# Two buffers for the last weight tiles, and another order of filter loads and reads, in a spectral filter and MLP mixer kernel

## The chip, the cores and the metric

The kernel runs on one core of one Trainium2 chip. The metric is the device time of one execution in microseconds (us), as a median of several executions. The engines of the core are TensorE (PE in the profile, with PEld for its weight loads), VectorE (DVE), ScalarE (ACT), GpSimd (POOL) and SyncE (SP). SP, ScalarE and GpSimd issue DMA transfers. [...]

## The reference

All arrays are float32 in the kernel; `x` is (8, 3008, 256). First a filter along the sequence, done in frequency space, then an MLP mixer: a token part over the 3008 positions and a channel part over the 256 channels.

```python
X = np.fft.rfft(x, axis=1)                       # n_freq = 1505
y = np.fft.irfft(X * (filt_r + 1j * filt_i)[None], n=3008, axis=1)

xt = y.transpose(0, 2, 1)
h = np.maximum(xt @ w_tok1, 0.0) @ w_tok2        # 3008 -> 256 -> 3008
u = y + h.transpose(0, 2, 1)
h2 = np.maximum(u @ w_ch1, 0.0) @ w_ch2          # 256 -> 1536 -> 256
out = u + h2
```

The weights arrive as 64-bit numbers and are turned into float32 on the chip.

## The kernel before, in words

**The filter.** The length 3008 is 47 x 64. For each batch, length-64 transforms are matmuls against a table `wa` or `was` (`a_unit`, `a_pair`); their results z are copied out of PSUM by ScalarE (L517) and written to a DRAM scratch `z_tmp` (L519). Then, for 16 chunks `c` of two frequencies, `b_pair` (L501 with `wb`) does the length-47 transforms from a tile `t2` of z read back (L601, L602), multiplies by the filter tile `filts[c % 3]` on VectorE (L644), `join` adds the parts (L649, L650), and `bi_pair` does the inverse (L501 again), whose result goes to another scratch, `g_tmp` (L659). The batches go through this in five groups: batch 0 alone, then (1, 2), (3, 4), (5, 6) and (7). Each group is a Python generator, `dft`, that yields after each small step. Where a group changes over from the length-64 steps to the chunks, GpSimd clears part of each filter tile (L664), and the first two chunks' reads, tables (L548) and filter pieces (L215, L217: eight small transfers from the two filter arrays) are issued on SP. In group (1, 2) the z results are written from ScalarE's queue and the x tiles lie partly in the filter tiles; in the later groups SP writes z.

**The mixer.** `mix` runs over batches, six column blocks `m` and six hidden blocks `jp`; one such item is an up projection in seven half-block products (`up_first` L844, `up_last` L860), sums on VectorE (`up_middle`, L822), a ReLU on ScalarE (L865) and a down projection (L878). In `up_middle` VectorE needs a copy `s` that ScalarE makes of the first product (L847). The steps of the next group's `dft` are called between the parts of these items, at places written out by hand. So the order of work on each engine is the order in which this Python code issues it.

**The weights.** Each weight tile is a generator of four steps, taken one each by four iterators over the same list `tiles`: load into a staging tile `st`, a copy with a scale on ScalarE (L265), two instructions on VectorE (L267, L268), and two more with the sum into the weight (L271, L273, L295). One `convert()` call advances the third iterator, then the fourth, then `copies()` advances the second as far as its rule lets it, then `fill` starts loads. At this stage the third iterator is one tile ahead of the fourth. The last ten tiles (`LAST`) are taken in the first five items of `mix`, one call ahead of `up_middle` and one ahead of `up_last` in each item. Their loads come from GpSimd's queue (L372, L383), between the sums that GpSimd makes of the finished weights (L362 to L366). Before the change each of these tiles holds one buffer of pool `p1p` (`top`) and one of `p2p` (`rest`), which the filter's products use later.

Of the kernel before, what the change touches and what calls it, by code (L numbers as in the profile page):

```python
# [10 lines left out]
FP32 = mybir.dt.float32  # L11
# [12 lines left out]
P = 128  # L24
# [95 lines left out]
def kernel(  # L120
# [30 lines left out]
    def pool(name, bufs, **kw):  # L151
        return ctx.enter_context(tc.tile_pool(name=name, bufs=bufs, **kw))
# [6 lines left out]
    p1p = pool("p1p", 1)  # L159
    p2p = pool("p2p", 1)  # L160
# [96 lines left out]
    def halves(st, n, pair):  # L257

        words = [st.bitcast(t).rearrange("p (n w) -> p n w", w=2)[:, 0:n] for t in (U32, FP32)]
        lo, hi, hi_f = words[0][:, :, 0], words[0][:, :, 1], words[1][:, :, 1]  # L260
        top, rest = (v[:, 0:n] for v in pair)
        top_i, rest_i = top.bitcast(U32), rest.bitcast(U32)


        nc.scalar.activation(out=top, in_=hi_f, func=AF.Copy, scale=2.0 ** -112)  # L265
        yield
        nc.vector.tensor_scalar(out=top_i, in0=top_i, scalar1=3, scalar2=None, op0=ALU.logical_shift_left)  # L267
        nc.vector.scalar_tensor_tensor(out=top_i, in0=hi, scalar=0x80000000, in1=top_i,  # L268
                                       op0=ALU.bitwise_and, op1=ALU.bitwise_or)
        yield  # L270
        nc.vector.tensor_scalar(out=rest_i, in0=top_i, scalar1=0xFF800000, scalar2=None, op0=ALU.bitwise_and)  # L271

        nc.vector.scalar_tensor_tensor(out=rest, in0=lo, scalar=2.0 ** -52, in1=rest, op0=ALU.mult, op1=ALU.mult)  # L273
        yield top, rest
# [3 lines left out]
    def spare_pair():  # L278
        where, tag = spare[0]
        spare.append(spare.pop(0))  # L280
        both = where.tile([P, 2, 512], FP32, tag=tag, name="both")
        return both[:, 0], both[:, 1]

    def rounded(st, n, parts, late):
        if late:

            pair = (p1p.tile([P, 512], FP32, tag="p1", name="top"), p2p.tile([P, 512], FP32, tag="p2", name="rest"))
        else:
            pair = spare_pair()
        h = halves(st, n, pair)  # L290
        yield next(h)
        yield next(h)
        top, rest = next(h)
        for src, dst in parts:
            nc.vector.tensor_tensor(out=dst, in0=src(top), in1=src(rest), op=ALU.add)  # L295


    ended = [0]
# [14 lines left out]
    def w1_load(i):  # L313
        st = stage(512)
        rows = moe_w_tok1.rearrange("(n2 n1) t -> n2 n1 t", n1=N1)
        q = nc.sync if i < EARLY else nc.gpsimd
        last = 2 * i + 2 == A
        if last:
            nc.gpsimd.memset(st.bitcast(U32)[HALF:P, 512:1024], 0)
        for h in range(2):  # L320
            n = 1 if last and h else 2
            lo = h * A + 2 * i
            src = rows[:, lo:lo + n, :]
            if h == 0:
                src = bass.AP(tensor=rows.tensor, offset=rows.offset + (A - 1 - lo) * DT,
                              ap=[[N1 * DT, N2], [-DT, n], [1, DT]])
            q.dma_start(st[h * HALF:(h + 1) * HALF, 0:n * DT].rearrange("p (a t) -> p a t", t=DT), src)
        yield

        h = halves(st, 512, spare_pair())  # L330
        yield next(h)
        yield next(h)
        on_chip(wai_t, *next(h), 512, [(lambda v: v, w1[:, 2 * i:2 * i + 2, :].rearrange("p a t -> p (a t)"))])

    def w2_load(i):

        t, g = divmod(i, W2G)
        nn = min(NG, N2 - g * NG)
        n = nn * N1

        st = stage(512)
        nc.gpsimd.dma_start(st[:, 0:n], moe_w_tok2[ts(t, P), ds(g * NG * N1, n)])
        yield
        dst = w2[:, t].rearrange("p (a h n2) -> p h n2 a", h=2, n2=HALF)[:, :, ds(g * NG, nn), :]

        def some(h, first, step, w):
            return (lambda v: bass.AP(tensor=v.tensor, offset=v.offset + first, ap=[v.ap[0], [N1, nn], [step, w]]),
                    dst[:, h, :, 0:w])

        parts = [some(0, A - 1, -1, A), some(1, A, 1, A - 1)]  # L350
        if i < BY_PE:
            h = halves(st, n, spare_pair())
            yield next(h)
            yield next(h)
            on_chip(ident, *next(h), n, parts)
        else:
            yield from rounded(st, n, parts, False)
# [10 lines left out]
    def wc1_load(i, late=True):  # L368
        c, q = divmod(i, DC // 512)
        st = stage(512)  # L370
        for g in range(CB):
            nc.gpsimd.dma_start(st[ts(g, CW)], moe_w_ch1[ds((g * DH + c) * CW, CW), ts(q, 512)])  # L372
        yield

        yield from rounded(st, 512, [(lambda v: v.rearrange("p (i j n) -> p i j n", j=2, n=P),
                           chan[0][:, 2 * q:2 * q + 2, slice(0, 5, 4) if c == 0 else slice(1, 7, 5)])], late)
        if c == DH - 1:
            for jp in range(2 * q, 2 * q + 2):
                combine(chan[0][:, jp:jp + 1])

    def wc2_load(i):
        st = stage(512)
        nc.gpsimd.dma_start(st.rearrange("p (j d) -> p j d", d=D),  # L383
                            moe_w_ch2[ts(i, 2 * P), :].rearrange("(j p) d -> p j d", p=P))
        yield

        def tile_of(dh):
            return lambda v: v.rearrange("p (j g e i) -> p e j g i", j=2, e=DH, i=CW)[:, dh]

        yield from rounded(st, 512, [(tile_of(dh), chan[1][:, i, n].rearrange("p j (g i) -> p j g i", i=CW))  # L390
                          for dh, n in ((0, slice(0, 2)), (1, slice(4, 7, 2)))], True)
        combine(chan[1][:, i:i + 1])


    LAST = ((wc2_load, 0), (wc1_load, 1), (wc1_load, 4), (wc2_load, 1), (wc1_load, 2), (wc2_load, 2), (wc1_load, 5),
            (wc2_load, 3), (wc2_load, 4), (wc2_load, 5))

    tiles = ([w1_load(i) for i in range(A // 2)] + [w2_load(i) for i in range(TC * W2G)]
             + [wc1_load(c * (DC // 512), False) for c in range(DH)] + [f(i) for f, i in LAST])
    begin, copy, middle, end = (iter(tiles) for _ in range(4))  # L400

    def advance(it):
        s = next(it, None)
        if s:
            next(s, None)
# [14 lines left out]
    def convert_end():  # L420
        ended[0] += 1
        advance(end)
        copies()
        fill(5)

    copied = [0]

    def copies():

        while copied[0] < len(tiles) and copied[0] <= ended[0] + (copied[0] < len(tiles) - len(LAST)):  # L430
            advance(copy)
            copied[0] += 1

# [101 lines left out]
    def dft(bs):  # L535
        first = bs[0] == 0
# [5 lines left out]
        def table_load(c):  # L542
            if c * KC % WC == 0:
                g = c * KC // WC
                where, tag = (t1p, "t1") if first and g % 5 > 2 else (wbp, "wb")
                shape, src = ([P, WC, P + KR], wbi0_d[:, ts(g, WC), :]) if first else ([P, 4, HALF], wbi_d[:, g])
                wbs[g] = where.tile(shape, FP32, tag=tag, name="wb")
                nc.sync.dma_start(wbs[g], src)  # L548

        def w_load(c):  # L550
            table_load(c)
            (filt_load if first else filt_pair)(c)
# [38 lines left out]
        def t2_load(c):  # L591
            if first:
                return
            t2s[c] = t2p.tile([P, KC, nb, D], FP32, tag="t2", name="t2")
            for h in range(2):
                z = z_d[place_of[bs[0]][0]].rearrange("(e h k) a b d -> e h a k b d", e=2, h=2)
                for e in range(2):
                    to = t2s[c][ds(h * HALF + e * A, A)]
                    k = c == 0
                    if k:  # L600
                        nc.sync.dma_start(to[:, 0:1], z[h, e, :, 0:1])  # L601
                    nc.sync.dma_start(to[:, k:KC], z[e, h, :, c * KC + k:c * KC + KC])  # L602
# [59 lines left out]
        for c in range(FB):  # L662
            if not first:
                nc.gpsimd.memset(filts[c][:, :, 0, :], 0.0)  # L664
            if c < 2:
                t2_load(c)
                if not first:
                    w_load(c)
        yield "w"
        yield "b"  # L670
        if not first:
# [365 lines left out]
    with tc.manual_schedule():  # L1037
        nc.sync.dma_start(wa0, wa0_d)
        nc.vector.memset(turned[:, A:K2, :], 0.0)
        for t in filts:  # L1040
            nc.vector.memset(t, 0.0)
        half = 0
        second = dft(GROUPS[1])
        for i, _ in enumerate(dft(GROUPS[0])):
            if i == 0:
# [33 lines left out]
        both = wcp.tile([P, 2, JP, 7, P], FP32, tag="wc", name="wc")  # L1079
# [76 lines left out]
```

## Time and profile before

| | |
|---|---|
| median of 3 runs | 2497.85 us (2496.29 to 2501.91) |
| the profiled execution | 2499.35 us |
| its span, first to last instruction | 2497.6 us |
| TensorE busy | 2420.1 us (97%) |
| VectorE busy | 1846.7 us (74%) |
| ScalarE busy | 678.6 us (27%) |
| GpSimd busy | 598.4 us (24%) |
| mean granted TensorE clock | 0.993 |
| DMA | 236.07 MB, mean 95 GB/s |

In lines of a timeline the columns are start, duration, engine, line, operation, output and inputs, shape and count, and in brackets the idle time of the engine just before, with what ended it. In lines of waits: who waited for whom, then total us, number, longest. In lines of stretches of time: the stretch, its length, busy us of PE, PEld, DVE, ACT and POOL with counts, the granted clock, the share of the DMA engines that was busy, and GB/s.

### The profile page before, as it was taken

The numbers are of one execution on the slowest core, as the hardware profiler recorded it, in microseconds if no ns is written. First come the engines' busy times: TensorE is split into PE (matmuls) and PEld (weight loads), VectorE is DVE, ScalarE is ACT, GpSimd is POOL, SyncE is SP. The second block draws the span as 40 slices with busy tenths as digits, with TensorE's granted clock in tenths as the row PEclk, the third lists the DMA queues.
The fourth block names the chain that finished last, engine by engine and source line by source line (L and its number), as shares of the span: only waits on it lengthen the run. The fifth ranks groups of instructions, "written<-read, shape, count | busy, mean of one in ns | idle before, by whom it ended". The sixth has DMA issues, their size and how long they took to land.

```text
span 2497.6 us, 33945 instructions
## 1 busy us (share of the span) xinstructions
PE 2420.1 (97%) x11836; PEld 1962.4 (79%) x11836; DVE 1846.7 (74%) x3404; ACT 678.6 (27%) x1348; POOL 598.4 (24%) x1086
## 2 busy tenths in 40 slices
PE   7888999999999999999999999999999999999997
PEld 3556676877788777887778877897888888898887
DVE  7686878587885878667885788758786678757776
ACT  5633222133221222223221222213221222212221
POOL 6473332212111211211121112111212112212121
PEclk9999999999999999999999999999999999999999
DMA  9973444254321222335332323314322121301100
GB/s 217 252 206 118 123 131 144 76 170 131 109 82 53 82 82 61 94 99 172 89 94 62 86 71 83 103 45 126 86 77 72 49 70 43 98 24 29 39 16 18
DMA packets 173122, 236.07 MB, mean 95 GB/s; under 512 B 33213, under 2 KB 123067, under 8 KB 172952
## 3 DMA queue, kind: packets, MB, share of 16 engines
q1 hardware_dynamic: 128344, 175.53, 24.1%
q0 software_dynamic: 33376, 48.46, 7.8%
q10 hardware_dynamic: 11232, 9.92, 1.3%
q8 instruction: 94, 1.54, 0.3%
q14 instruction: 76, 0.62, 0.1%
HBM read 156.56 MB, written 77.22 MB: 94 GB/s over the span
## 4 chain that ended last, share of the span: by engine, by line
PE 44%; DVE 5%; issue 1%; DMA 0%; ACT 0%; DVEq 0%; POOL 0%; SPq 0%; ACTq 0%; POOLq 0%
PE ps_po L878 17%; PE ps_pg L844 10%; PE ps_pg L860 7%; PE ps_b L721 2%; PE ps_acc L721 2%; PE ps_b L765 2%; PE ps_acc L765 2%; DVE t L822 1%; DVE hh L822 1%; PE ps_acc L501 1%; DVE p L644 1%; PE ps_b L501 1%; PE ps_b L743 1%; PE ps_acc L743 1%; DVE s L822 1%
## 5 line engine op out<-in xcount | busy, mean ns | idle before, releaser
L925 POOL DMA_DIRECT2D out_dram<-r x757 | 412.5, 553 | 1672.4 <-ACT hh L865 1408.4
L822 DVE TENSOR_TENSOR hh<-ps_pg,s 128x512 f32<-128x512 f32 (+3 forms) x864 | 482.6, 586 | 390.2 <-ACT s L847 386.8
L865 ACT ACTIVATE hh<-hh 128x512 f32<-128x512 f32 (+1 forms) x576 | 348.3, 623 | 986.2 <-DVE hh L822 986.2
L878 PE MATMUL ps_po<-t,wc 128*128 128x256 f32 (+1 forms) x2304 | 546.6, 380 | 4.2 <-DVE t L822 3.1
L878 PEld LDWEIGHTS ps_po<-t,wc 128*128 128x128 f32 x2304 | 426.3, 190 | 132.4 <-DVE t L822 41.1
L844 PE MATMUL ps_pg<-v,wc 128*128 128x256 f32 (+1 forms) x1728 | 415.5, 377 | 2.1 <-DVE v L822 2.1
L878 PE MATMUL ps_po<-hh,wc 128*128 128x256 f32 (+1 forms) x1728 | 413.5, 375 | 0.2 <-ACT hh L865 0.2
L844 PEld LDWEIGHTS ps_pg<-v,wc 128*128 128x128 f32 x1728 | 327.8, 191 | 43.5 <-DVE v L822 5.9
L878 PEld LDWEIGHTS ps_po<-hh,wc 128*128 128x128 f32 x1728 | 329.1, 191 | 38.2 <-ACT hh L865 0.5
L860 PE MATMUL ps_pg<-u,wc 128*128 128x256 f32 (+1 forms) x1152 | 295.8, 379 | 6.0 <-DVE hh L822 6.0
L860 PEld LDWEIGHTS ps_pg<-u,wc 128*128 128x128 f32 x1152 | 215.5, 190 | 63.7 <-DVE hh L822 30.5
L822 DVE TENSOR_TENSOR t<-t,hh 128x256 f32<-128x256 f32 (+1 forms) x576 | 245.2, 426 | 19.9
L822 DVE TENSOR_TENSOR s<-ps_pg,hh 128x512 f32<-128x512 f32 (+1 forms) x288 | 196.1, 681 | 30.3 <-DVE hh L822 0.5
L822 DVE TENSOR_TENSOR t<-hh 128x512 f32<-128x512 f32 (+1 forms) x288 | 192.9, 670 | 0.6 <-ACT hh L865 0.6
L847 ACT COPY s<-ps_pg 128x256 f32<-128x256 f32 (+1 forms) x288 | 106.2, 369 | 318.4 <-PE ps_pg L844 316.9
L844 PE MATMUL ps_pg<-u,wc 128*128 128x256 f32 (+1 forms) x576 | 173.8, 383 | 14.0 <-DVE hh L822 14.0
L860 PE MATMUL ps_pg<-v,wc 128*128 128x256 f32 (+1 forms) x576 | 168.8, 375 | 0.0
L844 PEld LDWEIGHTS ps_pg<-u,wc 128*128 128x128 f32 x576 | 105.6, 190 | 51.6 <-DVE hh L822 37.0
L860 PEld LDWEIGHTS ps_pg<-v,wc 128*128 128x128 f32 x576 | 109.3, 190 | 12.6
L822 DVE TENSOR_TENSOR u<-ps_b,u 128x256 f32<-128x256 f32 (+2 forms) x102 | 58.3, 572 | 67.5 <-PE ps_b L765 61.8
L822 DVE TENSOR_TENSOR u<-ps_acc,u 128x512 f32<-128x512 f32 (+2 forms) x108 | 62.4, 577 | 56.5 <-PE ps_acc L765 52.2
L721 PE MATMUL ps_b<-t,w 128*128 128x256 f32 x384 | 83.9, 380 | 8.1 <-DVE p L644 4.7
(140 smaller groups left out, 2464.7 us busy)
## 6 DMA issues: line engine op xcount, KB each, us to landing
w<-w_tmp SPq DMA_DIRECT2D x35, 896.0 KB
out_dram<-r POOLq DMA_DIRECT2D x698, 32.0 KB, 2.7
t<-g_tmp SPq DMA_DIRECT2D x42, 512.0 KB
g_tmp<-t SPq DMA_DIRECT2D x96, 192.0 KB
t<-z_tmp SPq DMA_DIRECT2D x180, 96.0 KB
z_tmp<-t SPq DMA_DIRECT2D x60, 256.0 KB
filt<-in_x_dram SPq DMA_DIRECT2D x90, 128.0 KB
wb<-wbi_t SPq DMA_DIRECT2D x64, 128.0 KB
```

Of the source, the lines that this page charges most:

```text
L501: nc.tensor.matmul(outs(i, j), stat(i, j), mov(i, j), start=True, stop=True)
L644: nc.vector.tensor_tensor(out=prods[c, h], in0=pss[h].unsqueeze(1).to_broadcast([P, 2, nb, D]), in1=filts[c % FB][:, :, 0, :].unsqueeze(2) ...
L721: nc.tensor.matmul(acc[:, t, :], w1[:, a, ts(t, P)], t4[b, a // TC4][:, a % TC4, :], start=(a == 0 and t == 0), stop=(a == A - 1 and t == ...
L743: nc.tensor.matmul(ps[:, ds(q * P, n)], t4[b, c][:, r, ts(dh, P)], wai[:, 0:n], start=(first and q == 0), stop=(not first and q == 3))
L765: nc.tensor.matmul(ps[:, ds(j * hw, hw)], h1[:, n, :], w2m[m % 2][:, at, 0:hw], start=(i < 2 and j == 0), stop=(j == len(todo) - 1))
L822: nc.vector.tensor_tensor(out=out, in0=in0, in1=in1, op=op)
L844: nc.tensor.matmul(ps[:, 0:hw], chan[0][:, jp, n, :], mov, start=True, stop=True)
L847: nc.scalar.copy(out=s[:, 0], in_=g[0][:, 0, 0:hw])
L860: nc.tensor.matmul(ps[:, 0:hw], chan[0][:, jp, n, :], mov, start=True, stop=True)
L865: nc.scalar.activation(out=hs, in_=hs, func=AF.Relu)
L878: nc.tensor.matmul(po[i][:, j, 0:hw], chan[1][:, jp, n, :], mov, start=(jp == 0 and first == 1), stop=(jp == JP - 1 and last == 1))
L925: q.dma_start(bass.AP(tensor=ob.tensor, offset=ob.offset + row * D + g * cw, ap=[[N1 * D, 32], [D if h else -D, n], [1, cw]]), blocks[ts(g ...
```

## The change

It has three parts. (1) The last ten weight tiles take both halves, `top` and `rest`, in one buffer of twice the size, from `p1p` and `p2p` in turn, so that two tiles are held at a time. (2) `copies()` lets ScalarE's copy run one call further ahead for these tiles too, as for all others. (3) At the changeover of groups after the first, the table and filter pieces of a chunk are issued ahead of the reads of z for that chunk; the clearing of the filter tiles comes before all of them, on GpSimd as before.

```diff
+    late_in = [(p2p, "p2"), (p1p, "p1")]
+
     def rounded(st, n, parts, late):
         if late:
 
-            pair = (p1p.tile([P, 512], FP32, tag="p1", name="top"), p2p.tile([P, 512], FP32, tag="p2", name="rest"))
+            late_in.reverse()
+            where, tag = late_in[0]
+            both = where.tile([P, 2, 512], FP32, tag=tag, name="both")
+            pair = both[:, 0], both[:, 1]
         else:
             pair = spare_pair()
...
     def copies():
 
-        while copied[0] < len(tiles) and copied[0] <= ended[0] + (copied[0] < len(tiles) - len(LAST)):
+        while copied[0] < len(tiles) and copied[0] <= ended[0] + 1:
             advance(copy)
             copied[0] += 1
...
         for c in range(FB):
             if not first:
                 nc.gpsimd.memset(filts[c][:, :, 0, :], 0.0)
-            if c < 2:
+        if not first:
+            for c in range(2):
+                w_load(c)
                 t2_load(c)
-                if not first:
-                    w_load(c)
         yield "w"
         yield "b"
```

## The prediction

> **What bounds the kernel now.** The page comes first: TensorE is busy 97%, and the chain that ended last, followed back over the second half, is 44% TensorE and 5% VectorE, so only TensorE's idle time can be won. The waits of TensorE (some 63 us in total) show where. By stretch of time, 15.3 us lie between 142 and 207 us, where the mixer starts beside the last ten weight tiles, and 5.0 us around 240 to 253 us, where the first batch group of the transform changes over from its length-64 stage to its length-47 stage. Waits of TensorE, then of VectorE, from 142 to 207 us:
>
> ```profile
> PE ps_pg L844 <- DVE hh L822: 9.3, 4, 2.8
> PE ps_pg L860 <- DVE hh L822: 6.0, 3, 3.0
> DVE top L267 <- ACT top L265: 11.3, 10, 1.6
> ```
>
> TensorE waits for VectorE alone, and VectorE for one thing: ScalarE's copy of a weight tile (L265). The timelines of ScalarE and VectorE show the ring:
>
> ```profile
> 150.22 0.66 ACT L265 ACTIVATE top<-st 128x512 f32<-128x512 f32 x1 [2.53 <-DVE wc L295]
> 150.78 0.36 ACT L847 COPY s<-ps_pg 128x256 f32<-128x256 f32 x1
> ```
> ```profile
> 149.29 0.89 DVE L295 TENSOR_TENSOR wc<-top,rest 128x256 f32<-128x256 f32 x2
> 150.91 0.43 DVE L267 TENSOR_SCALAR top<-top 128x512 uint32<-128x512 uint32 x1 [0.73 <-ACT top L265]
> ...
> 161.88 0.43 DVE L267 TENSOR_SCALAR top<-top 128x512 uint32<-128x512 uint32 x1 [1.63 <-ACT top L265]
> ```
>
> VectorE's last use of a tile (L295) frees the single top/rest pair, ScalarE fills it (L265), VectorE may go on (L267): 0.73 us idle where ScalarE is free, 1.6 us where it first ends two copies and DMA issues of the transform (L517, L519). The changeover, from the timelines of SP, TensorE, VectorE and from the stretches of time (clock before the DMA share):
>
> ```profile
> 237.98 0.30 SPq L601 DMA_DIRECT2D t<-z_tmp  x1
> ...
> 240.77 0.36 SPq L602 DMA_DIRECT2D t<-z_tmp  x1
> 241.18 0.35 SPq L548 DMA_DIRECT2D wb<-wbi_t  x1
> ...
> 244.34 0.25 SPq L217 DMA_DIRECT2D filt<-in_filt_i_dram  x1
> ```
> ```profile
> 243.31 0.71 PE L501 MATMUL ps_b<-t,wb 48*64 48x512 f32 x2 [1.93 <-DMA filt<-in_filt_r_dram]
> ...
> 252.70 1.62 PE L501 MATMUL ps_b<-p,wb 64*64 64x512 f32 x3 [3.05 <-DVE p L649]
> ```
> ```profile
> 249.47 1.23 DVE L644 TENSOR_TENSOR p<-ps_b,filt 128x1024 f32<-128x1024 f32 x1 [5.96 <-DMA wb<-wbi_t]
> ```
> ```profile
> 254.00:258.00 4.00, 4.00 (x21) 1.76 (x14) 2.77 (x6) 1.39 (x3) 0.64 (x2) 0.69 0.66 206
> ```
>
> SP stands until 237.98 for the last z write, issues eight reads, and only then the table and eight filter loads that needed no z. TensorE waits 1.93 us for the table (L501 takes only reads and table, L644 the filter, so the releasers named are neighbours of the true ones); the product (L644) waits until 249.47 for the filter, whose last part was issued at 244.34; TensorE waits 3.05 us for the product, and then runs slowly (clock 0.69). The three later changeovers look different: there the filter waits for POOL, and TensorE never stands:
>
> ```profile
> 615.65 0.36 SPq L602 DMA_DIRECT2D t<-z_tmp  x1
> 616.06 0.35 SPq L548 DMA_DIRECT2D wb<-wbi_t  x1
> 626.16 0.30 SPq L215 DMA_DIRECT2D filt<-in_filt_r_dram  x1
> ```
> ```profile
> 625.59 1.47 POOL L664 MEMSET filt<- 128x512 f32 x3
> ```
> ```profile
> 637.02 0.65 PE L501 MATMUL ps_acc<-t,wb 48*64 48x512 f32 x2
> ```
>
> [...] Here the clock is 0.69 from 254 to 258 us, after 3.05 us idle. [...] L268 takes 0.69 or 0.83 us here; both orders run it beside GpSimd's sums, so I charge nothing for that.
>
> **Part 1, the tiles.** Call a tile's steps A (L265), B (L267, L268) and C (L271, L273, L295). In the old program a call issues A(n+1), C(n), B(n+1) with A waiting for C. In the new one it issues B(n+1), C(n), A(n+2): B has its data already, but A(n+2) shares its buffer with C(n) and waits for it. Nothing is added. In calls ahead of the ReLUs, VectorE goes straight on to L822: the 0.73 vanishes. In calls ahead of `up_middle`, ScalarE's s copy (L847), which VectorE needs next, stands behind A in its queue. That is the late thing next: L295 ends 150.18, A 150.22, s 150.78 to 151.14, plus 0.03, so 0.99 us from C to L822. The idle times in order and their successors: 1.22 (no gain, the u copy ends later), 0.73 to 0.99, 0.73 to 0, 1.63 to 0.99, 0.73 to 0, 1.61 to 0.99, 0.73 to 0, 1.63 to 0.99, 0.73 to 0, 1.57 to 0 (the last item has no A left). The sum is -0.26 + 4 x 0.73 + 0.64 + 0.62 + 0.64 + 1.57 = 6.1 us. TensorE's waits at the same places (2 to 3 us per item at L844, 1.5 at the last L860) let this through. One load is tight: tile 34's four pieces are issued at 166.56 to 168.60 behind GpSimd's sums, about 0.8 later when C comes after B, and land 3.9 us (median of L372's transfers) after the last starts, near 172.9, when A wants them at 172.5: some 0.5 us. GpSimd's sums for L878 end within 0.3 us of need twice. I take **5.0 us**. Bounds: not more than 10.1 (all waits but the first), not less than -2 (every A ahead of an s copy waiting for its load).
>
> **Part 2, first changeover.** SP's 30 transfers come in a new order: table, eight filter pieces, eight reads for chunk 0, then the same of chunk 1 with four reads; POOL's order is the same. The table and filter 0 need no z: memset 0 ends at 228.2 (L664, 227.64 + 0.53), so they issue from there to about 231.5, in time that SP idles, beside the last z writes (DMA share 0.3 there). The reads stay at 237.98 to 241.13, as z does. TensorE starts when the last read is in; it was issued 0.41 us before the old table, so 242.9 for 243.31. Products: 243.6 + 2 x 1.2 + 2 x 0.68 = 247.4. TensorE's own work up to the inverse stage ends at 249.65 - 0.4 = 249.2, so the 3.05 wait goes, with 1.8 us to spare. Old: inverse 252.70, next forward stage 257.28. New: 249.2 + 1.02 + 1.40 (the same steps at 263.25, 264.27 and 265.67, full clock) = 251.6. Gain **5.6 us**: 0.4 + 3.05 and 2.1 of slow clock. Chunk 1's table, filter and reads now run 241.2 to 246.3 and are wanted from 251.6. Bounds: 0.4 (a new wait takes the 3.05) to 6.5 (the first wait shrinks to 0.5).
>
> **Part 3, later changeovers.** Eight reads move behind the memset: from 612.86-616.0 to 629.0-633.3 (filter 0 ends 629.03; in the program each transfer waits for the one eight before it, and the last filter piece, issued at 628.78, held SP until 632.94, as it will hold the eighth read). TensorE wants them at 637.02. In the other two the eighth read is issued at 1222.20 for 1226.03 and at 1763.62 for 1766.46. The read issued at 240.77 was in by 243.31, so 2.54 us is a bound: slack 1.5, 1.3 and 0.3. Cost 0, hidden behind TensorE's mixer work up to there; if a read takes as long as that filter piece (4.2 us), 0.1, 0.4 and 1.4 us. Bounds: 0 to 3 us lost; no gain, as TensorE doesn't wait there. The weights and t4 reads behind (L784, L715) go 3.3 us later, tens of us ahead of use.
>
> **Sum.** 2499.35 (profiled; span 2497.6 and 1.75 around it) - 5.0 - 5.6 = 2488.7. The median shown is 1.5 lower, so 2497.85 - 10.6 = **2487.3**.
>
> **Rivals.**
> - Only the changeover pays: A, two tiles ahead, blocks ScalarE's s copies and ReLUs as long as the old wait. For it: A still waits for C. Against: B leaves the ring. 2492 (minus 5.6), from 2490 to 2494.
> - Only the tiles pay: the reads, not the filter, were what the product waited for. Against: reads were consumed at 243.3. 2493.
> - The later changeovers eat the gain with 3 to 4 us each, slow clock included: 2497.
> - Slower: the reads behind POOL's stores and memset. If the last read lands 3.5 us after TensorE wants it, the stall costs what the first changeover's did (5.6 us with the slow clock), 17 for three, less 10.6: 2504. It decides from 3.5 us lost at each (10.6 in three), a stall of about 2 us with the slow clock's share; that takes reads of 5 to 6 us. The trace shows 2.5 for reads and 4.5 for filter pieces.
>
> **How the numbers follow.** 0.2% (5 us) is about what a measurement of this kernel can tell. Both pay: 0.66, 2484 to 2490. Changeover alone 0.14, tiles alone 0.06, eaten up 0.06, slower 0.08. Faster 0.78 (the first, and 0.12 of the next two), same 0.14, slower 0.08. The range 2483.5 to 2495.5 leaves out the last two and a little on either side.
>
> **What would show it.** From 142 to 205 us L267 waits for ScalarE at no call; L822 waits about 1 us for L847 at four; TensorE's 15.3 us fall to about 10. L215 of the first changeover stands near 229 us, L644 starts near 243.6, the 3.05 wait is gone and the clock stays 1.00. Later, L501 starts unhindered. I am wrong if ScalarE's L265 waits for `st` loads, if L501 waits for `z_tmp` reads, or if L501's 3.05 stays.

## The result, and the profile after

The changed kernel takes 2492.7 us (median of 10 executions, 2488.72 to 2494.92) against 2497.41 us for the kernel before on the same chip (10 executions, 2495.74 to 2501.91). The ratio is 0.9977, with an interval of 0.9968 to 0.9987: a gain of 5.7 us by the ratio and 4.7 by the medians, where 10.6 were forecast. Two repeats gave 0.9974 and 0.9972 (below). The profiled execution took 2492.05 us (span 2490.3, clock 0.995), 7.3 less than the profiled one before.

From L300 on, the changed kernel's line numbers are five higher than in the kernel before: L822 is now L827, L847 is L852, L501 is L506, L644 is L649, L878 is L883. L265 to L273 and L215, L217 keep their numbers.

**The tiles.** Waits of TensorE, then of VectorE, from 142 to 207 us of the changed kernel:

```profile
PE ps_pg L849 <- DVE hh L827: 5.0, 4, 1.6
PE ps_pg L865 <- DVE hh L827: 4.6, 3, 3.2
PE ps_po L883 <- POOL wc L371: 2.5, 3, 1.9
PE ps_b L756 <- ACT t L522: 0.2, 1, 0.2
```
```profile
DVE hh L827 <- ACT s L852: 4.4, 4, 1.4
DVE both L267 <- ACT both L265: 1.5, 1, 1.5
```

The ten waits of L267 for ScalarE, 11.3 us, are gone. (The one of 1.5 us that stands there is that of the last tile ahead of the ten, which did not wait in the kernel before.) Four waits for the copy of `s` have come in their place, as the prediction had it: 0.99, 0.99, 1.41 and 1.00 us. TensorE's waits fell from 15.3 to 12.3 us, not to 10: 2.5 us of them are new, for GpSimd's sums. ScalarE's timeline shows the queueing at two of the four, VectorE's one of the results, and TensorE's the new wait:

```profile
152.91 0.66 ACT L265 ACTIVATE both<-st 128x512 f32<-128x512 f32 x1 [3.63 <-DVE wc L300]
153.48 0.36 ACT L852 COPY s<-ps_pg 128x256 f32<-128x256 f32 x1
...
174.68 0.67 ACT L265 ACTIVATE both<-st 128x512 f32<-128x512 f32 x1 [1.70 <-DMA st<-in_moe_w_ch_dram]
175.26 0.35 ACT L852 COPY s<-ps_pg 128x256 f32<-128x256 f32 x1
```
```profile
153.87 0.42 DVE L827 TENSOR_TENSOR hh<-ps_pg,s 128x256 f32<-128x256 f32 x1 [0.99 <-ACT s L852]
```
```profile
174.60 1.13 PE L883 MATMUL ps_po<-hh,wc 128*128 128x256 f32 x4 [1.95 <-POOL wc L371]
```

The copy at 152.91 had to wait for VectorE's last use of the buffer, and the copy of `s` comes right behind it. The one at 174.68 waited 1.70 us for its tile's load (tile 34), where the prediction allowed 0.5; that is the 1.41 us among the four waits. The prediction had named a wait of L265 for a load as a sign of being wrong, and this one sign came true.

**The first changeover.** SP's timeline, then TensorE's, VectorE's and a stretch of time (the clock stands before the DMA share):

```profile
224.43 0.30 SPq L215 DMA_DIRECT2D filt<-in_filt_r_dram  x1
...
227.09 0.25 SPq L217 DMA_DIRECT2D filt<-in_filt_i_dram  x1
234.54 0.30 SPq L606 DMA_DIRECT2D t<-z_tmp  x1
...
237.32 0.37 SPq L607 DMA_DIRECT2D t<-z_tmp  x1
```
```profile
237.54 1.18 PE L506 MATMUL ps_b<-t,wb 48*64 48x512 f32 x4
238.89 1.38 PE L506 MATMUL ps_acc<-t,wb 48*64 48x512 f32 x4 [0.17 <-DMA t<-z_tmp]
...
245.15 0.65 PE L506 MATMUL ps_b<-p,wb 64*64 64x512 f32 x2
```
```profile
239.67 1.19 DVE L649 TENSOR_TENSOR p<-ps_b,filt 128x1024 f32<-128x1024 f32 x1
```
```profile
245.00:249.00 4.00, 4.00 (x25) 1.80 (x24) 2.67 (x6) 2.01 (x4) 2.81 (x6) 1.00 0.63 192
```

The filter pieces go out 7 us and more ahead of the first read. The product L649 no longer waits for them (5.96 us before), the inverse stage follows at 245.15 without the 3.05 us wait, and the clock stays at 1.00. At this point the changed kernel is some 3.8 us ahead; with that taken off, the predicted times (product 243.6, inverse 249.2, next forward stage 251.6) are 239.8, 245.4 and 247.8, and the trace has 239.67, 245.15 and 247.66.

**The later changeovers.** SP and TensorE at the second one:

```profile
621.24 0.25 SPq L217 DMA_DIRECT2D filt<-in_filt_i_dram  x1
621.53 0.30 SPq L606 DMA_DIRECT2D t<-z_tmp  x1
...
625.17 0.29 SPq L607 DMA_DIRECT2D t<-z_tmp  x1
```
```profile
629.50 0.65 PE L506 MATMUL ps_acc<-t,wb 48*64 48x512 f32 x2
```

The reads now stand behind the filter, the last one of the first chunk at 625.17, and TensorE takes them at 629.50 with no wait; nor is there one at the other two (last read 1214.24 for 1218.79, and 1756.52 for 1759.20).

### The profile page after: what moved, and what is told of

Its sections match the earlier page's. It is cut to its first block, busy times and chain, and to the rows that moved or that the text cites. A ratio compares the mean times of both kernels' runs of the same rounds, so it can differ in the third digit from the quotient of the medians.

```text
span 2490.3 us, 33936 instructions
## 1 busy us (share of the span) xinstructions
PE 2418.7 (97%) x11836; PEld 1959.8 (79%) x11836; DVE 1847.9 (74%) x3404; ACT 677.4 (27%) x1348; POOL 598.6 (24%) x1086
## 4 chain that ended last, share of the span: by engine, by line
PE 44%; DVE 5%; issue 1%; ACT 0%; DMA 0%; SPq 0%; DVEq 0%; POOL 0%; ACTq 0%; POOLq 0%
PE ps_po L883 17%; PE ps_pg L849 10%; PE ps_pg L865 7%; PE ps_b L726 2%; PE ps_acc L726 2%; PE ps_b L770 2%; PE ps_acc L770 2%; DVE t L827 1%; DVE hh L827 1%; PE ps_acc L506 1%; DVE p L649 1%; PE ps_b L506 1%; PE ps_acc L748 1%; PE ps_b L748 1%; DVE s L827 1%
## 5 line engine op out<-in xcount | busy, mean ns | idle before, releaser
L827 DVE TENSOR_TENSOR hh<-ps_pg,s 128x512 f32<-128x512 f32 (+3 forms) x864 | 482.6, 586 | 395.7 <-ACT s L852 391.7
L883 PE MATMUL ps_po<-t,wc 128*128 128x256 f32 (+1 forms) x2304 | 546.6, 380 | 4.2 <-DVE t L827 3.1
L883 PEld LDWEIGHTS ps_po<-t,wc 128*128 128x128 f32 x2304 | 426.3, 190 | 132.3 <-DVE t L827 41.7
L883 PE MATMUL ps_po<-hh,wc 128*128 128x256 f32 (+1 forms) x1728 | 413.2, 375 | 2.7 <-POOL wc L371 2.5
L883 PEld LDWEIGHTS ps_po<-hh,wc 128*128 128x128 f32 x1728 | 327.8, 190 | 41.2 <-POOL wc L371 3.7
L827 DVE TENSOR_TENSOR t<-t,hh 128x256 f32<-128x256 f32 (+1 forms) x576 | 246.0, 427 | 19.8
L827 DVE TENSOR_TENSOR s<-ps_pg,hh 128x512 f32<-128x512 f32 (+1 forms) x288 | 196.1, 681 | 30.3 <-DVE hh L827 0.5
L827 DVE TENSOR_TENSOR t<-hh 128x512 f32<-128x512 f32 (+1 forms) x288 | 193.8, 673 | 0.6 <-ACT hh L870 0.6
L852 ACT COPY s<-ps_pg 128x256 f32<-128x256 f32 (+1 forms) x288 | 106.0, 368 | 315.9 <-PE ps_pg L849 313.8
L827 DVE TENSOR_TENSOR u<-ps_b,u 128x256 f32<-128x256 f32 (+2 forms) x102 | 58.3, 572 | 67.5 <-PE ps_b L770 61.8
L827 DVE TENSOR_TENSOR u<-ps_acc,u 128x512 f32<-128x512 f32 (+2 forms) x108 | 62.4, 577 | 56.5 <-PE ps_acc L770 52.2
```

Of the source, the lines that this page charges most:

```text
L827: nc.vector.tensor_tensor(out=out, in0=in0, in1=in1, op=op)
L852: nc.scalar.copy(out=s[:, 0], in_=g[0][:, 0, 0:hw])
L883: nc.tensor.matmul(po[i][:, j, 0:hw], chan[1][:, jp, n, :], mov, start=(jp == 0 and first == 1), stop=(jp == JP - 1 and last == 1))
```

## The experiments

**How they are read.** Beside the times, every trace was cut at the same five landmarks: the start of the token sums (the 96 matmuls of L721), the first token product after the late tiles (L751, at 206.66 us in the kernel before), and VectorE's second sum of an item (L822, `s`) in the 9th, 14th and 32nd item of the mixer. So the tiles, the changeover and the chunks behind it each have a stretch of their own. Each row is one profiled execution (us):

| kernel | token sums to end of tiles | to item 9 | changeover: items 9 to 14 | items 14 to 32 | the rest |
|---|---|---|---|---|---|
| before | 88.64 | 32.24 | 51.22 | 159.83 | 2047.65 |
| after | 84.48 | 32.72 | 46.22 | 161.09 | 2047.86 |
| e0, after again | 85.19 | 32.71 | 46.86 | 160.63 | 2047.54 |
| e9, after, third | 85.16 | 32.72 | 46.41 | 159.56 | 2047.35 |
| e1, new order alone | 90.01 | 32.23 | 46.63 | 159.74 | 2047.67 |
| e2, tiles alone | 84.43 | 32.71 | 50.08 | 160.38 | 2047.25 |
| e3, two buffers alone | 85.16 | 32.23 | 49.54 | 159.39 | 2047.40 |
| e4, buffers and order | 85.81 | 32.23 | 46.63 | 160.09 | 2047.34 |
| e5, after, no sums | 84.83 | 32.71 | 45.82 | 158.95 | 2049.16 |
| e6, before, no sums | 88.31 | 32.22 | 50.17 | 158.96 | 2047.12 |
| e7, end first | 82.31 | 32.36 | 46.04 | 160.34 | 2047.47 |
| e8, copy behind s | 81.28 | 32.23 | 46.81 | 159.71 | 2047.29 |
| e10, sums moved | 80.42 | 32.22 | 45.43 | 158.80 | 2047.28 |
| e11, loads first | 80.67 | 32.22 | 45.83 | 159.05 | 2047.29 |

The time ahead of the token sums, which no kernel here changes, runs from 114.0 to 118.6 us in these traces. That alone can cover the gain, so medians and stretches are compared, not spans.

### The parts, one at a time (e0 to e3; one chip, kernel before 2498.68 us)

e0 is the changed kernel again.

> The changed kernel a second time, beside the one before on one chip. In the first pair of traces the stretch of the weight tiles gained 5.9 us and the first changeover 5.0, but 1.7 us had been lost ahead of both (the 96 matmuls of the token sums took 22.64 us for 20.96, the same work at a lower clock) and 2.1 us were lost in the chunks after the changeover. Theory A (the losses are chance[...]): 4 to 10 us faster, the token sums take 21.0 or 22.6 us from one trace to the next whatever the kernel. Theory B (the losses belong to the change): again 4 to 5 us faster, token sums again 22.6 us, chunks again 2 us slower.

2491.27 us, ratio 0.9974 (0.9965 to 0.9983). The token sums took 23.47 us here, 22.64 in e1, whose only change comes behind them, and 20.96 in the changed kernel's third trace (e9): their length is chance, as theory A has it, and not a price of the change.

e1 has the new order of the changeover, and the tiles of the kernel before:

```diff
-            if c < 2:
+        if not first:
+            for c in range(2):
+                w_load(c)
                 t2_load(c)
-                if not first:
-                    w_load(c)
```

> The kernel before with part 3 alone (table and filter pieces ahead of the reads). Theory A (parts add up): TensorE's 1.93 and 3.05 us at the first changeover go, 4 to 6 us faster. Theory B (what the changeover gains is given back in the chunks behind it, where VectorE's steps meet GpSimd's sums): 2 to 3 us faster, with new waits of L501 for VectorE between 260 and 460 us. Rival C (the reads stand behind POOL's memset at later changeovers): no faster, L501 waiting for z_tmp near 637, 1226 and 1766 us.

2494.54 us, ratio 0.9986 (0.9978 to 0.9993): 3.5 us, between what theories A and B had. Its changeover takes 46.63 us, as in the changed kernel. Part of theory B's give-back is there (below, at e5 and e6).

e2 has the two buffers and the copy further ahead, and the old order of the changeover:

```diff
-            pair = (p1p.tile([P, 512], FP32, tag="p1", name="top"), p2p.tile([P, 512], FP32, tag="p2", name="rest"))
+            late_in.reverse()
+            where, tag = late_in[0]
+            both = where.tile([P, 2, 512], FP32, tag=tag, name="both")
+            pair = both[:, 0], both[:, 1]
...
-        while copied[0] < len(tiles) and copied[0] <= ended[0] + (copied[0] < len(tiles) - len(LAST)):
+        while copied[0] < len(tiles) and copied[0] <= ended[0] + 1:
```

> The kernel before with parts 1 and 2 alone (two buffers, copies one call further ahead). Theory A: 5 to 6 us faster, all of it between 142 and 207 us. Rival D (the tiles' gain depends on the load order or is given back at the changeover, where TensorE then waits longer for z): 0 to 2 us faster, and TensorE's waits at the first changeover above 5.0 us.

2493.21 us, ratio 0.9974 (0.9965 to 0.9983): 6.5 us by the ratio, 5.5 by the medians. Its trace has the old order of the changeover, and shows what the old order costs. TensorE's timeline of e2, then its stretch from 236 to 250 us:

```profile
237.00 0.83 PE L506 MATMUL ps_b<-t,wb 48*64 48x512 f32 x2 [2.43 <-DMA filt<-in_filt_r_dram]
...
239.12 3.78 PE L883 MATMUL ps_po<-t,wc 128*128 128x256 f32 x8
```
```profile
236.00:250.00 14.00, 13.00 (x52) 8.08 (x52) 7.45 (x13) 2.20 (x5) 9.89 (x18) 0.76 0.60 174
```

After the wait of 2.43 us the clock is low (0.76 over the stretch), and eight matmuls that take 1.99 us in the changed kernel take 3.78. No wait for the product follows: the eight matmuls took 1.79 us more, and the product was there when the inverse stage began at 246.61 us. The four traces of the old order line up: the longer the eight matmuls take, the shorter the wait for the product. They take 1.99, 3.05, 3.25 and 3.78 us in the kernel before, e6, e3 and e2, and the waits are 3.05, 1.56, 0.96 and 0 us. Only in the kernel before did the full wait come, with a slow clock behind it (0.69 from 254 to 258 us); the others had their slow clock ahead of the product, in the time of the wait (from 236 to 250 us 0.88 in e6 and e3, 0.76 in e2). Their changeovers last 51.22, 50.17, 49.54 and 50.08 us.

e3 has the first hunk of e2's diff alone: two buffers, ScalarE's copies as far ahead as before.

> The kernel before with the two buffers alone, copies as before: ScalarE's copy of the next tile no longer waits for VectorE's last use of this one. Theory E (it is the buffer that pays; the copy one call further ahead gives back 1 us at each s copy): VectorE's five 0.73 us waits go, the 1.6 us ones stay, because there ScalarE is busy with the transform's copies: 3 to 4 us faster. If the further copy is what pays: within 1 us of before. If both buffers alone free all of it: 8 to 10 us faster.

2493.05 us, ratio 0.998 (0.9972 to 0.9988): 5.0 us, more than was expected of it. VectorE's waits for ScalarE's copies from 142 to 207 us are halved in number by the second buffer alone (five times, 8.4 us), and the stretch of the tiles takes 85.16 us:

```profile
DVE both L267 <- ACT both L265: 8.4, 5, 2.7
```

### Where the rest of the gain went (e4 to e6; kernel before 2496.18 us)

e4 is e3 with e1's order.

> Two buffers and the new order of the first changeover, ScalarE's copies no further ahead than before. If the parts add up as their stretches did in the four kernels profiled so far: the weight tiles 57.4 us (5.2 less than before), the stretch from the tiles to the next forward stage about 45.2 (5.4 less). If the give-back in the chunks up to 450 us belongs to the number of us gained ahead of them (it fell on both kernels that have both parts), the time is 6 to 8 us under before, 2490 to 2492 against 2497.5; if each part keeps its own gain as measured alone (3.5 and 5), 8 to 9 us under it.

2490.06 us, ratio 0.9974 (0.9966 to 0.9982): 6.1 to 6.5 us, and no different from the changed kernel. **The copy further ahead brought nothing that these runs can tell.** In the traces it takes 0.7 us off the tiles (85.16 to 84.43 from e3 to e2) and gives 0.5 back at once: the kernels with that rule as the change has it (after, e0, e2, e5, e9) take 32.71 us to item 9, those without it 32.23. There the second product of the pair at L756 follows the first by 3.01 us and not 2.61, and 0.2 us of this is the wait in the last line of TensorE's waits shown above (L756 for ScalarE's L522).

e5 and e6 test a suspicion: items 14 to 32 are slower in the changed kernel's first trace than before. From the changeover on GpSimd makes sums of the second token weights (L797, L792 before), and VectorE's instructions that meet them take longer (1.70 us for 0.89 below). VectorE, GpSimd and TensorE in the changed kernel, then GpSimd and VectorE in the kernel before, all between items 9 and 14:

```profile
267.01 1.70 DVE L827 TENSOR_TENSOR t<-t,hh 128x256 f32<-128x256 f32 x2
```
```profile
266.58 1.84 POOL L797 TENSOR_TENSOR w<-w 128x256 f32<-128x256 f32 x2 [4.54 <-DMA w_tmp<-w]
```
```profile
273.97 1.15 PE L506 MATMUL ps_b<-p,wb 64*64 64x512 f32 x3 [0.49 <-DVE p L654]
```
```profile
269.22 1.52 POOL L792 TENSOR_TENSOR w<-w 128x256 f32<-128x256 f32 x2 [4.68 <-DMA w_tmp<-w]
```
```profile
274.14 0.42 DVE L822 TENSOR_TENSOR hh<-ps_pg,s 128x256 f32<-128x256 f32 x1 [7.32 <-ACT s L847]
```

The pair of VectorE sums takes 0.89 us elsewhere, GpSimd's pair 1.53. In the changed kernel the two meet and take 1.70 and 1.84, and TensorE then waits 0.49 us for the product that VectorE makes a little later. In the kernel before, GpSimd's pair fell into 7.32 us in which VectorE was idle. e5 and e6 leave these sums out (the stores stay), e5 from the changed kernel and e6 from the one before:

```diff
         def t13():
-            sub(b22, b22, b12)
-            sub(b12, b12, b11)
+            pass
 
         def t24():
-            nc.gpsimd.tensor_tensor(out=b11, in0=b22, in1=b11, op=ALU.add)
-            sub(b21, b11, b21)
+            pass
```

> The changed kernel without the four sums that GpSimd makes of each block of the second token weights (t13 and t24 of w2_sums are left out; the stores to DRAM stay), so that these sums can lengthen no VectorE instruction between 250 and 450 us. Theory: about 3 us of the predicted gain are given back where GpSimd's sums meet VectorE's in other places than before. Then this kernel is 2 to 4 us faster than the changed one (2487 to 2489), and against its twin, the kernel before without the same sums, it gains 10 to 11 us, the 10.6 of the prediction's sum. Rival: the give-back is something else (DMA, clock, chance); then the pair differ by 6 to 7.5 us as the full kernels do.

2488.23 us, ratio 0.9968 (0.9956 to 0.9981).

> The kernel before without GpSimd's sums of the second token weights (t13 and t24 of w2_sums left out, the stores stay): the twin of the changed kernel without them. Theory: the sums cost it little, since they fell into VectorE's waits or were caught up later: 0 to 2 us faster than before, 2496 to 2498. Rival: it gains the same 2 to 4 us as the other, and the difference between the two stays at 6 to 7.5 us.

2495.67 us, ratio 0.9999 (0.9991 to 1.0007). The pair differs by 7.4 us, nearer to the rival's 6 to 7.5 than to 10 to 11; but the two intervals reach 3.1 and 2.0 us to either side, so the times alone do not exclude the theory. The traces tell more. From item 14 to 32 both take 158.95 us, the same to 0.01, where kernels with the sums scatter from 158.80 to 161.09: the meetings of the two engines cost between nothing and some 2 us there, and which it is changes from kernel to kernel. The profiled pair differs by 1.26 us.

Inside the changeover a part of the cost recurs. From the third chunk's forward transforms (TensorE's L501 on `t2`) to the fourth's, the four kernels with the old order take 14.77 or 14.78 us. The eight with the new order and the sums in their old place take 15.31 to 15.85, and in each TensorE waits 0.2 to 0.8 us for VectorE as above. e5, without the sums, takes 14.76, and so does e10 to 0.01, which has them in another place. **So the new order pays 0.5 to 1.1 us here to GpSimd's sums**, which the old order did not.

e5's last stretch is 1.3 us and more longer than all others because the 96 matmuls of its third batch's token sums took 22.67 us and not 20.99, behind a wait of 2.07 us. Five other traces have the same wait there and no such loss; in the changed kernel's first one the clock in the 5 us behind it is 1.00.

### Past the change (e7 to e11)

e7 takes the waits for `s` away. A call ends tile n on VectorE first, so that ScalarE's copy runs beside the upper half of the next tile, in both places in `mix`:

```diff
             if ended[0] < len(tiles):
-                convert()
+                convert_end()
+                convert_middle()
```

> The changed kernel with the two halves of a late tile's call in the other order: a call ends tile n on VectorE (L271, L273, L300), lets ScalarE copy tile n+2 (L265) beside it, and only then makes the upper half of tile n+1 (L267, L268). Theory: VectorE's waits for the copy of s (L852: 0.99, 0.99, 1.41, 1.00 us) go, as ScalarE's copy of the tile runs while VectorE makes the upper half, and GpSimd's sums (2.5 us of TensorE's wait) start 0.9 us earlier: the weight tiles take 52 to 54 us instead of 56.7, and the time is 2 to 5 us below the changed kernel. Rival: tile 34's load and the product chain set the pace, then 56 us and no difference.

2487.83 us, ratio 0.9966 (0.9954 to 0.9979), on the chip of e4 to e6. Of the four short waits one is gone and two are shorter (0.83 and 0.68 us), but one load is late, and the copy waiting for it holds up the copy of `s`, so that the fourth has become 4.03 us. ScalarE and VectorE in e7:

```profile
163.56 0.66 ACT L265 ACTIVATE both<-st 128x512 f32<-128x512 f32 x1 [1.68 <-DMA st<-in_moe_w_ch_dram]
164.12 0.36 ACT L852 COPY s<-ps_pg 128x256 f32<-128x256 f32 x1
```
```profile
164.51 0.42 DVE L827 TENSOR_TENSOR hh<-ps_pg,s 128x256 f32<-128x256 f32 x1 [4.03 <-ACT s L852]
```

The tiles (from the second L748 group to L756, the measure of its expectation) took 56.23 us, not 52 to 54. e8 issues ScalarE's copy after that of `s`, or after the ReLUs; `convert_end(False)` leaves `copies()` out:

```diff
-                convert_end()
+                convert_end(False)
                 convert_middle()
...
                 up_middle(hhs[i], w, g, s)
+            copies()
...
                 up_last(jp, uts[b, m], vts[b, m], w, g, s, hhs[i])
+            copies()
```

> The kernel whose calls end tile n first (e7), with ScalarE's copy of tile n+2 issued only after the copy of s (L852 there) or the ReLUs of the call, so that a copy that waits for its tile's load no longer holds up the products. In e7's trace one such wait of 1.68 us held the copy of s and VectorE idled 4.03 us there. Theory: that wait falls to about 2 us and the shorter waits for the copy of s go, so the weight tiles take 53 to 55 us instead of 56.2, and the time is 1 to 3 us below e7. Rival: the tiles' loads, or the products' own chain over VectorE, set the pace; then 55.5 to 57 us again and no difference to e7.

2484.74 us, ratio 0.9949 (0.9936 to 0.9962; kernel before 2498.07 us, as for e9 to e11). VectorE's waits for the copy of `s` from 144 to 203 us, in e8:

```profile
DVE hh L828 <- ACT s L853: 2.1, 4, 0.8
```

They were 5.5 us in e7, and the tiles take 53.51 us. That measure starts behind the token sums, which took 22.64 us here and 20.96 in e7. With them, as in the table, e8 is only 1.0 us ahead of e7 (81.28 and 82.31), and the times of the two, 4 us apart by the ratios with intervals of some 3 us on each, do not settle what moving the copy is worth. **The two steps together are faster than the changed kernel**: e8 is 13 us by the ratio below the kernel before, and 5.8 below the changed kernel of the same chip, e9:

> The changed kernel a third time, to see how far its ratio to the kernel before is the same from one set of runs to the next (0.9977 and 0.9974 so far). Expected 0.9970 to 0.9980, 5 to 7.5 us below the kernel before; the weight tiles 56.6 to 56.9 us in its trace, as in its two others, and the time up to the end of the token sums anywhere within 138 to 141 us.

2490.53 us, ratio 0.9972 (0.9963 to 0.9982). The ratio is as expected; the traced stretches are not. The token sums ended at 134.96 us and the tiles took 59.08 us. What is steady is their sum. With the token sums in 20.96 us (e5 and e9; the clock of e9 is 1.00 from 118 to 140 us) the tiles take 58.75 and 59.08; with them slower (22.5 to 23.5 us, in after, e0 and e2) the tiles take 56.6 to 56.85; from the start of the token sums to the end of the tiles all five take 84.4 to 85.2. With the old tiles it is not: 88.64 and 88.31 behind sums of 20.96 us (before, e6), 90.01 in the one trace with slower ones (e1, 22.64 us).

e10 was run on e8, not on e7 as its text has it, and takes up GpSimd's sums behind the first part of an item.

> e7 with GpSimd's sums and stores of the second token weights (w2_sums) taken up at the start of an item, behind the first part of its products, rather than at its end. Theory: where GpSimd's sums meet VectorE's instructions decides what they cost (2.5 to 2.7 us between kernels with and without them, from the changeover to 450 us); with them elsewhere the stretch from 284 to 450 us changes by up to 1.5 us either way. Rival: GpSimd starts them when the stores of before them have landed, whatever their place in the order, and nothing moves (within 0.3 us).

2485.05 us, ratio 0.9948 (0.9936 to 0.9960). Items 14 to 32 take 158.80 us, as without sums, but e11, whose sums are where they were, takes 159.05. So that stretch does not tell whether the place matters. The changeover does: there TensorE's wait behind the sums is gone, as said at e5 (14.77 us, for 15.69 in e8 and 15.58 in e11). In the time of the whole kernel, which is e8's, so little is not seen.

e11 is e8 with GpSimd's five sums of a finished tile put behind the next loads (those of `chan[0]` in the same way):

```diff
-        combine(chan[1][:, i:i + 1])
+        put_off.append(chan[1][:, i:i + 1])
...
         fill(5)
+        while put_off:
+            combine(put_off.pop(0))
```

> e8 with the loads of later tiles issued ahead of GpSimd's five sums of the tile just ended, not behind them. Theory: a load then starts up to 4.6 us earlier, ScalarE's wait for a tile's load (1.68 us in e7, 1.70 in the changed kernel) goes, while the sums start 0.8 to 2 us later and hold the products up by up to 2 us in all: the weight tiles take 52 to 55 us. Rival: the later sums cost more than the earlier loads bring, 56 to 58 us.

2484.92 us, ratio 0.9950 (0.9938 to 0.9962); tiles 54.51 us. No different from e8. From 142 to 207 us TensorE waits 4.8 us for VectorE instead of 9.1, and 3.8 us for GpSimd's sums of the tiles, for which it did not wait in e8. But e10, where these sums stand as in e8, waits 3.3 us for them too, so the exchange cannot be put down to their new place.

## Why the prediction was right, and its size wrong

The direction and the main mechanisms held; the gain was 5.7 to 7.0 us over three sets of runs, not 10.6. The first median, 2492.7 us, lies above the 2484 to 2490 that the prediction gave to its own case, and inside its wider range only. By stretches, with means over the kernels that share a part:

- **Part 1, 5.0 us forecast: 3.7 found.** The old tiles take 89.0 us from the start of the token sums (before, e1, e6), the new ones 84.8 (after, e0, e2, e5, e9): 4.2. All of it is idle time of TensorE, whose 278 matmuls there take 72.8 us on average before and 72.9 after. With so few traces this is good to about 1 us: where the token sums took 20.96 us the gain is 3.5, and where they took 22.64 us (e1, after) it is 5.5. The copies further ahead then cost 0.5 behind the tiles, a price that the prediction did not have. The exchange of waits was right to a hundredth at three of the four places (0.99 us). Two terms were mis-sized: tile 34's load, 0.5 us allowed and 1.6 to 3.2 waited in the five traces, and GpSimd's sums, said to end in time, for which TensorE waited 1.9 to 2.5 us. One trace misleads here: behind the token sums the profiled pair gains 5.85 us, but 2.7 of this is the same 182 matmuls at a clock of 1.00 and not 0.95, and the token sums ahead took 1.7 us more, at a clock of 0.93 from 118 to 142 us for 1.00 before.
- **Part 2, 5.6 us forecast: 3.8 found.** Up to the next forward stage the new side came out within 0.3 us at each step. Two terms failed. First, the old side was one execution, and the longest of four: from item 9 to the next forward stage it takes 18.39 us, in e2, e3 and e6 17.20, 16.70 and 17.35. The prediction added 3.05 us of wait and 2.1 us of slow clock as if both recurred; in the other three the slow clock (0.76 to 0.88 from 236 to 250 us) came in the time of the wait. That is 1.0 us. Second, 0.9 us are given back behind that stage: from there to item 14 the old order takes 32.8 to 32.9 us in all four, the new one 33.2 to 34.7, on average 33.8 (after, e0, e1, e4, e5, e9). In part this is VectorE meeting GpSimd's sums (1.70 us for 0.89 at 267 us of the changed kernel). The prediction had the tiles' L268 beside GpSimd's sums and charged nothing for it; it had no term for such meetings here. Over both steps, 50.25 us became 46.43.
- **Part 3, 0 forecast: 0 found.** From the issue of the last read to its use 2.7 to 4.6 us pass, and TensorE does not wait.
- **What the prediction did not have:** 0.6 us lost in items 14 to 32 (160.43 over after, e0 and e9, 159.79 over before and e1), within their scatter, so that it may be chance.

The sum is 4.2 - 0.5 + 3.8 - 0.6 = 6.9 us. Of the rivals, "only the changeover pays" lies nearest the first median (2492), but e2 and e3 exclude it: the tiles alone bring 5 to 6.5 us. Later changeovers eat nothing, so the slower case falls too. That each part alone brings more by its ratio (3.5 and 6.5) than is left when both are made is not settled: the difference is within the intervals.

## What to carry to other kernels

When a stall ends in a slow clock, price it from several executions: in three of four traces here the slow clock came in the time of the later wait (0 to 1.56 us left of it, for 3.05) instead of on top of it, and the worst of the four promised more than the change could give. What matters after a buffer is added is what stands behind the instruction that now waits, as the copy of `s` stood behind the tile's copy (1.68 us of waiting in ScalarE, 4.03 in VectorE, in e7): here the second buffer gave all the gain that could be told, the copy further ahead nothing, and ending a tile first, with that copy behind the short one that the products need (e7, e8), gave about as much again. Measure a stage over a stretch that takes in the changes of clock ahead of it, not only over the window in which its waits are seen, and count TensorE's idle and busy time apart. And work that comes earlier can run beside other work than before, as VectorE's sums ran beside GpSimd's here (1.70 us for 0.89): ask what that costs.

## What the runs showed of the hardware

- **A low clock followed some waits of about 2 us, and not others.** At the old changeover, the eight matmuls after a wait of 1.93 us (before) took 1.99 us, after 2.26 (e3) 3.25, after 2.31 (e6) 3.05, after 2.43 (e2) 3.78. In all 14 traces from 100 us on, the mean clock of the 5 us behind a wait of TensorE was below 0.95 in none of 150 cases of 0.7 to 1.8 us, in 6 of 22 of 1.8 to 2.2 us, and in 19 of 27 longer ones.
- **The same 96 matmuls took 20.96 us in some executions and up to 23.9 in others**: 20.96 behind a wait of 3.34 us in the kernel before, with a clock of 1.00 from 118 to 142 us, and 22.64 behind one of 3.35 in the changed one, with 0.93. With the new tiles it cost nothing that shows up to their end (84.4 to 85.2 us with either).
- **GpSimd's and VectorE's sums took longer where they met.** At 267 us of the changed kernel VectorE's pair took 1.70 us, for 0.89 elsewhere, and GpSimd's 1.84, for 1.52 at 269 us of the kernel before, where VectorE was idle.
